# Block 0 of a fused S5 and GEGLU kernel: tile 3 moved last and read from its DMA-turned form, the last weight chunk split by columns over two DMA queues

## The chip, the cores and the metric

The kernel runs on one core of a Trainium2 chip. The metric is the device time of one execution in microseconds, the median of several runs. A profile of one execution adds a span, from the first to the last instruction, which is a little shorter than that execution's device time.

The core has five engines that run side by side and meet at semaphores: TensorE (PE, matmuls; its weight loads are listed as PEld), VectorE (DVE), ScalarE (ACT), GpSimd (POOL) and SyncE (SP), which here does nothing but issue DMAs. ScalarE can issue DMAs as well. Each issuing engine has its own queue; 16 DMA engines move the packets.

## The reference

```
xn = layernorm(x)                                  # x: 2048 x 512, bf16
Lam_bar = exp(dt * Lam);  B_bar = ((Lam_bar - 1) / Lam)[:, None] * B
Bu = xn @ B_bar.T;  h[t] = Lam_bar * h[t-1] + Bu[t]           # complex, 512 states
y  = 2 * real(h @ C.T) + xn * Dskip
g  = (gelu(xn @ w_gate) * (xn @ w_up)) @ w_down    # 512 -> 1376 -> 512
out = x + y + g
```

## The kernel before

The 2048 rows are worked in four blocks of 512 rows, a block in four tiles of 128 rows. For each block there are these stages on TensorE: GU (gate and up products, L843, and L817 for the last 96 columns), BU (input to the states, L749), DN (down product and states to output, L885). VectorE does the recurrence (scans), ScalarE evacuates PSUM, applies gelu and makes the tables.

TensorE contracts over the partition dimension, so a normalized tile must be turned (rows and columns exchanged) before it is used. There are two ways in this kernel. `TR` (L733 to L738) issues a DMA transpose per tile from SyncE: `XN[tile]` becomes columns 128j to 128j+127 of `XNT[block]`, and the buffers `XTk[block][j]` stand for that in the dependency tracking. `cent_T` (L678 to L689) turns a tile on TensorE with an identity matrix and ScalarE copies it out of PSUM into `XC_all`; it is used in block 0 alone, where there is no time to wait for DMAs.

Block 0's start is special. The tiles are only centred (mean subtracted; `cent` for tiles 0 and 1, `sub` for 2 and 3), turned by `cent_T`, and multiplied with the weights before the row's scale is known. The scale 1/std is applied later, as a per-row scalar, when PSUM is evacuated (`GT_evac`: a gelu with `scale=sc` on ScalarE, then a product with the scalar `sc` on VectorE, giving rows of `H0`). Here rows are on partitions: the tile is the stationary operand, and gate and up columns of both weights stream together (`WGU`). The columns 0 to 895 are cut in four units u, `FR = ((0,256),(256,512),(512,768),(768,896))`. For units 0 and 1 of tiles 0 to 2, `GT_k` (L701) adds one row block k of the weights at a time, in the order in which these land. The remaining ten pairs (j, u) of tile and unit are whole groups, `GT_mm` (L712), in an order written out by hand at L1013: (3,0), (3,1), (0,2), (0,3), (1,2), (1,3), (2,2), (2,3), (3,2), (3,3), each with a PSUM bank of its own from a second list. Each is followed by its `GT_evac`. Later `H0_T` turns `H0` by DMA. Columns 896 to 1375 of block 0 (ft 7 to 10) are done by `GU(0, [7, 8, 9, 10], halved=[7])` on the DMA-turned tiles; ft 7 is cut in halves over the tiles (0, 1 and 2, 3), so that its first half needs only two of the turns. `norms` (L634) makes the fully normalized tiles for these turns on VectorE.

The weights `WG` and `WU` come in column chunks `FC = [(0,512), (512,896), (896,1376)]`. The first chunk is loaded by row blocks k (`ld_wk`, L488, eight copies of 128 rows). The others are one copy for each matrix, with 512 packets (`ld_w`, L493). `wdeps` maps a column tile ft to the chunk it has to wait for.

The order on SyncE at the start is: x tiles and first weight chunk, second weight chunk, third weight chunk, a small transpose of the parameters (`tr_par`, L515), the four turns of block 0 (L736), x of block 1 (L482), turns of B_re and B_im straight from memory (L526), the Dskip row (L535), x of block 2 (L482), the turns of block 1 (L736), and so on.

All instructions are recorded with their buffers, and a list scheduler (`Sched`) orders VectorE, ScalarE and GpSimd by a cost model. TensorE and SyncE are kept in the recorded order. `order_behind` ties one instruction behind another on the same engine. `next_bank` deals out the eight PSUM banks in turn; `rstate["n"]` is its counter.

Of the kernel before, what the change touches and what calls it, by code (L numbers as in the profile page):

```python
# [9 lines left out]
ALU = mybir.AluOpType  # L10
ACTF = mybir.ActivationFunctionType
# [350 lines left out]
def d_act(n, ptr=0): return 190.0 + 0.833 * n + 90.0 * ptr  # L362
# [3 lines left out]
def build(nc, ins, out):  # L366
    with ExitStack() as es:
# [13 lines left out]
        assert WG.lo == 0 and WU.lo == WG.hi  # L381
        WGU = arena_t[:, 0:2 * KD * F].rearrange("p (w k f) -> p w k f", w=2, k=KD)
        WD = A.alloc("WD", [KF, D], BF16)
        FC = [(0, 512), (512, 896), (896, F)]
        WGc = [Buf("WGc%d" % i, "sbx", 10 * i, 10 * i + 1) for i in range(KD + 2)]
        WUc = [Buf("WUc%d" % i, "sbx", 100 + 10 * i, 101 + 10 * i) for i in range(KD + 2)]
        wdeps = lambda Wc, ft: Wc[0:KD] if ft < 4 else [Wc[KD + (ft > 6)]]
        WDc = [Buf("WDc%d" % i, "sbx", 200 + 10 * i, 201 + 10 * i) for i in range(2)]
        XNT_all = A.alloc("XNT", [NB, KD, TB_], BF16)
        XNT = ring(XNT_all, "XNT", NB)  # L390
# [100 lines left out]
        def ld_w(W, Wc, src, n):  # L491
            f0, f1 = FC[n]
            return S.dma(lambda e: e.dma_start(W.ap[:, :, f0:f1], src[:, f0:f1].rearrange("(k p) f -> p k f", p=128)),  # L493
                         1024 * (f1 - f0), writes=[Wc[KD + n - 1]], tag="ld_w")
# [5 lines left out]
        for k in range(KD):  # L500
# [1 line left out]
                ld_x0(k)  # L502
            ld_wk(WG, WGc, ins["B_w_gate"], k)
            ld_wk(WU, WUc, ins["B_w_up"], k)
        ld_w(WG, WGc, ins["B_w_gate"], 1)
        ld_w(WU, WUc, ins["B_w_up"], 1)

        def load_par():
            for q, nm in enumerate(("A_log_dt", "A_Lambda_re", "A_Lambda_im")):
# [17 lines left out]
                      1.4 * 512 * 1024, writes=[b_], tag="tr_" + nm, issue=3000.0)  # L527

        def load_W():
            ld_w(WG, WGc, ins["B_w_gate"], 2)  # L530
            ld_w(WU, WUc, ins["B_w_up"], 2)

        def load_B():
            load_T([A.sub(BBT_all, "BBTc%d" % c, c) for c in range(2)], ("A_B_re", "A_B_im"))
# [169 lines left out]
        def GT_mm(j, u, bank):  # L704
            f0, f1 = FR[u]
            w = f1 - f0
            dst = PS[bank][:, 0:2 * w].rearrange("p (w f) -> p w f", w=2)

            def f(e):
                ins_ = None  # L710
                for k in range(KD):
                    ins_ = e.matmul(dst, XCd(j, k), WGU[:, :, k, f0:f1], start=(k == 0), stop=(k == KD - 1))  # L712
                return ins_
            PE(f, d_pe([2 * w] * KD), wdeps(WGc, 2 * u) + wdeps(WUc, 2 * u) + XCs[j], [BANK[bank]], "GT")

        def GT_evac(j, u, bank):
            f0, f1 = FR[u]
            w = f1 - f0
            GATE["nh"] = kk = (GATE["nh"] + 1) % 3
            sc, rb = rss[j]  # L720
            GATE["last_gelu"] = S.order_behind(ACT(lambda e: e.activation(GG[kk].ap[:, 0:w], PS[bank][:, 0:w], ACTF.Gelu_apprx_tanh, scale=sc),  # L721
                                                   d_act(w, 1), [BANK[bank], rb], [GG[kk]], "gelu"), GATE.get("last_gelu"))
            hp = Buf("H0_%d_%d" % (j, u), "sb", H0[j].lo + 2 * f0, H0[j].lo + 2 * f1)
            GATE["hm"] = S.order_behind(V(lambda e: e.scalar_tensor_tensor(H0[j].ap[:, f0:f1], PS[bank][:, w:2 * w], sc, GG[kk].ap[:, 0:w], ALU.mult, ALU.mult),  # L724
                                          d_dve_1x(w), [BANK[bank], GG[kk], rb], [hp], "hmul"), GATE.get("hm"))

        def H0_T():
            for j in range(4):
# [77 lines left out]
        def GU_rest(b):  # L806
            k2, ft = b % 2, KF - 1
            f0, m = 128 * ft, FROWS[ft]
            for i in range(2):
                bank = next_bank()  # L810

                def f(e, i=i, bank=bank):
                    ins_ = None
                    for j in (2 * i, 2 * i + 1):
                        dst = PS[bank][:, 256 * (j % 2):256 * (j % 2) + 2 * m].rearrange("p (w f) -> p w f", w=2)
                        for dk in range(KD):
                            ins_ = e.matmul(dst, XNT[b].ap[:, dk, 128 * j:128 * (j + 1)], WGU[:, :, dk, f0:f0 + m],  # L817
                                            start=(dk == 0), stop=(dk == KD - 1))
                    return ins_
                PE(f, d_pe([2 * m] * 8), [WGc[KD + 1], WUc[KD + 1]] + XTr(b), [BANK[bank]], "GR%d" % b)  # L820
# [171 lines left out]
        ch(*stats(0, 1))  # L992
        op, mn0, qb0, rq0 = root(0, 0, 3)
        ch(op)
        ch(*stats(0, 3)); ch(sub(3))
        ch(recip(qb0, rq0))
        op, mn3, qb3, rq3 = root(0, 3, 4)
        ch(op)
        rss = [(rq0.ap[:, i:i + 1], rq0) for i in range(3)] + [(rq3.ap, rq3)]
        for j in range(2):  # L1000
            ch(norms(0, [j], mn0, rq0, 0))
        ch(recip(qb3, rq3))
        TR(0, [0, 1])
# [107 lines left out]
```

## Time and profile before

| what | value |
|---|---|
| median of 3 runs | 177.13 us (177.06 to 177.36) |
| the profiled execution: its time | 177.26 us |
| its span | 175.9 us |
| granted TensorE clock | 1.000 |
| bytes moved by DMA | 14.36 MB in 32421 packets |

In the lines of the profile an engine's name with a q (SPq, ACTq) marks the issue of a DMA. The duration of such a row is how long the issue held the engine's queue, not how long the transfer took. A row of the timeline gives start, duration, engine, source line, operation, output and input, count, and in brackets the idle time ahead of it with what ended it. "arena" is the one SBUF allocation in which all buffers lie, so "arena<-arena" with DMA_TRANSPOSE is a turn within SBUF. The matmul durations of the profile overlap each other: consecutive 512-column matmuls start 0.216 us apart, 256-column ones 0.109 us.

### The profile page before, as it was taken

The page shows a single profiled execution, that of the slowest core. Times are in us where ns is not written, and L with a number is a line of the kernel's source. Part 1 is how long each engine was busy: PE and PEld are TensorE (multiplying, and loading weights), DVE is VectorE, ACT ScalarE, POOL GpSimd, SP SyncE. Part 2 cuts the span into 40 slices and gives each one's busy share as a digit, 9 for nine tenths or more (in the row PEclk, how much of TensorE's full clock was granted, in tenths as well). Part 3 has the DMA queues.
Part 4 walks back from the last instruction along what each step waited for, and adds up shares of the span by engine and source line. Part 5 has one row for each costly group of instructions (what it writes and reads, how often), then busy time and mean ns, then how long its engine had stood idle before and what let it go on. Part 6 is the DMA issues. An engine that isn't in the chain of part 4 may idle for free.

```text
span 175.9 us, 2549 instructions
## 1 busy us (share of the span) xinstructions
PE 172.8 (98%) x903; PEld 85.4 (49%) x903; DVE 159.7 (91%) x279; ACT 95.8 (54%) x187; POOL 10.7 (6%) x24
## 2 busy tenths in 40 slices
PE   7999999999999999999999999999999999999995
PEld 2645664744544444444644444444464444444454
DVE  6797999987999989889899999989999899999941
ACT  5367668999766899383676793000667970000000
POOL 3132120211000000002200000000000000000000
DMA  5999989975899000002015000002004000000311
GB/s 144 281 322 154 216 136 203 174 132 114 162 270 270 11 0 2 0 30 75 18 33 112 5 0 4 0 0 89 30 0 34 0 0 0 0 0 4 119 62 60
DMA packets 32421, 14.36 MB, mean 82 GB/s; under 512 B 23737, under 2 KB 32409, under 8 KB 32409
## 3 DMA queue, kind: packets, MB, share of 16 engines
q1 hardware_dynamic: 31952, 13.84, 36.9%
q10 hardware_dynamic: 456, 0.36, 0.6%
q8 instruction: 7, 0.11, 0.3%
q14 instruction: 6, 0.04, 0.1%
HBM read 6.46 MB, written 2.10 MB: 49 GB/s over the span
## 4 chain that ended last, share of the span: by engine, by line
PE 95%; DMA 2%; SPq 1%; issue 0%; DVE 0%
PE PS L885 37%; PE PS L843 32%; PE PS L749 16%; PE PS L712 4%; PE PS L817 3%; PE PS L701 2%; DMA arena<-in_B_w_up_dram 2%; SPq L488 1%; PE PS L684 0%; SPq L497 0%; DVE arena L903 0%
## 5 line engine op out<-in xcount | busy, mean ns | idle before, releaser
L885 PE MATMUL PS<-arena 128*128 128x512 bf16 (+3 forms) x323 | 66.2, 366 | 0.0
L843 PE MATMUL PS<-arena 128*128 128x512 bf16 (+1 forms) x272 | 58.1, 373 | 0.0
L885 PEld LDWEIGHTS PS<-arena 128*128 128x128 bf16 (+1 forms) x323 | 30.8, 98 | 35.2
L843 PEld LDWEIGHTS PS<-arena 128*128 128x128 bf16 x272 | 26.5, 98 | 29.5
L787 DVE TENSOR_TENSOR_SCAN arena<-arena 128x512 bf16<-128x512 f32 x32 | 38.9, 1256 | 0.0
L859 ACT ACTIVATE arena<-PS 128x512 bf16<-128x512 f32 x33 | 19.8, 599 | 26.2 <-DVE arena L903 16.7
L749 PE MATMUL PS<-arena 128*128 128x512 bf16 (+1 forms) x144 | 28.3, 355 | 0.1
L863 ACT ACTIVATE arena<-PS 128x512 bf16<-128x512 f32 x33 | 19.8, 599 | 5.4 <-PE PS L843 5.4
L749 PEld LDWEIGHTS PS<-arena 128*128 128x128 bf16 x144 | 14.0, 98 | 13.7 <-DMA arena<-arena 0.6
L877 ACT ACTIVATE PS<-arena 128x512 f32<-128x512 bf16 (+2 forms) x17 | 9.6, 582 | 19.7 <-DVE arena L903 19.0
L758 ACT ACTIVATE arena<-PS 128x512 bf16<-128x512 f32 x32 | 17.6, 597 | 1.6 <-PE PS L749 1.6
L903 DVE TENSOR_TENSOR arena<-PS,arena 128x512 bf16<-128x512 f32 (+2 forms) x17 | 10.9, 654 | 6.4 <-PE PS L885 6.4
L865 DVE TENSOR_TENSOR arena<-arena 128x512 bf16<-128x512 bf16 x33 | 13.2, 419 | 2.1 <-ACT arena L863 2.0
L776 DVE TENSOR_TENSOR arena<-arena 128x4096 bf16<-128x4096 bf16 (+1 forms) x5 | 9.2, 1859 | 0.4 <-ACT arena L611 0.4
L799 DVE TENSOR_TENSOR arena<-arena 128x4096 bf16<-128x4096 bf16 x4 | 9.2, 2291 | 0.1
L774 DVE TENSOR_TENSOR arena<-arena 128x4096 bf16<-128x4096 bf16 (+1 forms) x5 | 9.2, 1861 | 0.0
L800 DVE TENSOR_TENSOR arena<-arena 128x4096 bf16<-128x4096 bf16 x4 | 9.1, 2287 | 0.0
L615 DVE BATCH_NORM_STATS2 arena<-arena 128x6 f32<-128x512 bf16 x12 | 7.8, 685 | 0.9 <-DMA arena<-in_A_x_dram 0.7
L721 ACT ACTIVATE arena<-PS,arena 128x256 bf16<-128x256 f32 (+1 forms) x16 | 6.5, 450 | 3.3 <-DVE arena L621 1.5
L712 PE MATMUL PS<-arena 128*128 128x512 bf16 (+1 forms) x40 | 7.1, 336 | 0.0
L701 PE MATMUL PS<-arena 128*128 128x256 bf16 (+1 forms) x36 | 6.2, 308 | 0.2 <-DMA arena<-in_B_w_up_dram 0.2
L724 DVE SCALAR_TENSOR_TENSOR arena<-PS,arena 128x256 bf16<-128x256 f32 (+1 forms) x16 | 6.2, 444 | 0.0
(95 smaller groups left out, 124.2 us busy)
## 6 DMA issues: line engine op xcount, KB each, us to landing
out_dram<-arena SPq DMA_DIRECT2D x15, 128.0 KB, 1.7
arena<-in_A_x_dram SPq DMA_DIRECT2D x3, 512.0 KB, 6.3
arena<-in_B_w_down_dram SPq DMA_DIRECT2D x1, 1280.0 KB, 8.8
arena<-in_B_w_gate_dram SPq DMA_DIRECT2D x4, 128.0 KB, 3.4
arena<-in_B_w_up_dram SPq DMA_DIRECT2D x4, 128.0 KB, 3.6
arena<-in_B_w_gate_dram SPq DMA_DIRECT2D x1, 480.0 KB, 6.8
arena<-in_B_w_up_dram SPq DMA_DIRECT2D x1, 480.0 KB, 7.6
arena<-arena SPq DMA_TRANSPOSE x25, 3.3
```

What stands on the lines that cost most here:

```text
L701: PE(lambda e: e.matmul(dst, XCd(j, k), WGU[:, ws[0]:ws[-1] + 1, k, f0:f1], start=first, stop=k == KD - 1, skip_group_check=True), d_pe([w ...
L712: ins_ = e.matmul(dst, XCd(j, k), WGU[:, :, k, f0:f1], start=(k == 0), stop=(k == KD - 1))
L749: ins_ = e.matmul(PS[bank][:, 128 * j0:128 * j1], BBT[c][dk].ap[:, 128 * s:128 * (s + 1)], XNT[b].ap[:, dk, 128 * j0:128 * j1], start=(dk ...
L758: GATE["evBu"] = ACT(lambda e, bank=bank, k3=k3, s=s, c=c: e.activation(SSc[k3][s][c].ap, PS[bank][:, :], ACTF.Copy), d_act(512), [BANK[ba ...
L787: V(lambda e, g=g, rb=rb, init=init: e.tensor_tensor_scan(g.ap, rb, g.ap, init, ALU.mult, ALU.add), d_dve_scan(512), [g, PA[RRr]] + ([CARc ...
L843: ins_ = e.matmul(PS[bank][0:m, c0:c1], W.ap[:, dk, 128 * ft:128 * ft + m], XNT[b].ap[:, dk, c0:c1], start=(dk == 0), stop=(dk == KD - 1))
L859: GATE["last_gelu"] = ACT(lambda e, bg=bg, kk=kk, m=m: e.activation(GG[kk].ap[0:m, :], PS[bg][0:m, :], ACTF.Gelu_apprx_tanh), d_act(512), ...
L863: ACT(lambda e, bu=bu, kk=kk, m=m: e.activation(UPB[kk].ap[0:m, :], PS[bu][0:m, :], ACTF.Copy), d_act(512), [BANK[bu]], [UPB[kk]], "evU")
L865: V(lambda e, kk=kk, m=m, ft=ft, k2=k2: e.tensor_tensor(HTt[k2][ft].ap[0:m, :], GG[kk].ap[0:m, :], UPB[kk].ap[0:m, :], ALU.mult), d_dve_tt ...
L877: ACT(lambda e: e.activation(PS[bank][:, c0:c1], X[tt].ap[:, c0:c1], ACTF.Copy), d_act(c1 - c0), [X[tt]], [BANK[bank]], "seed")
L885: ins_ = e.matmul(PS[bank][:, c0:c1], l_[:, 128 * j:128 * (j + 1)], r_[:, c0:c1], start=False, stop=last and n == len(ops) - 1, skip_group ...
L903: V(lambda e: e.tensor_tensor(OUTB[ko].ap[:, c0:c1], PS[bank][:, c0:c1], XD[tt].ap[:, c0:c1], ALU.add), d_dve_1x(c1 - c0), [BANK[bank], XD ...
```

## The change

In block 0 tile 3 is no longer centred and turned on TensorE. It is normalized fully, turned by DMA, and its four groups read it from `XNT[0]` at the end of the order; so its gelu and product take no scale. The order of the ten groups becomes (0,2), (1,2), (2,2), (0,3), (1,3), (2,3), (3,0), (3,1), (3,2), (3,3), with other banks. The DMA turns of block 0 are issued in the order 0, 3, 1, 2. The weight columns from 512 on are cut in four chunks instead of two: 512 to 767, 768 to 895, 896 to 1023, 1024 to 1375. The first three are loaded from SyncE ahead of the small transpose and the turns (six copies, where there were four); the last, of both matrices, is issued from ScalarE's queue behind the gelu of group (2,2).

```diff
-        FC = [(0, 512), (512, 896), (896, F)]
+        FC = [(0, 512), (512, 768), (768, 896), (896, 1024), (1024, F)]
-        wdeps = lambda Wc, ft: Wc[0:KD] if ft < 4 else [Wc[KD + (ft > 6)]]
+        wdeps = lambda Wc, ft: Wc[0:KD] if ft < 4 else [Wc[KD + (ft > 5) + (ft > 6) + (ft > 7)]]
...
-        ld_w(WG, WGc, ins["B_w_gate"], 1)
-        ld_w(WU, WUc, ins["B_w_up"], 1)
+        for n in (1, 2):
+            ld_w(WG, WGc, ins["B_w_gate"], n)
+            ld_w(WU, WUc, ins["B_w_up"], n)
...
         def load_W():
-            ld_w(WG, WGc, ins["B_w_gate"], 2)
-            ld_w(WU, WUc, ins["B_w_up"], 2)
+            ld_w(WG, WGc, ins["B_w_gate"], 3)
+            ld_w(WU, WUc, ins["B_w_up"], 3)
...
                 for k in range(KD):
-                    ins_ = e.matmul(dst, XCd(j, k), WGU[:, :, k, f0:f1], start=(k == 0), stop=(k == KD - 1))
+                    xs = XCd(j, k) if j < 3 else XNT[0].ap[:, k, 128 * j:128 * (j + 1)]
+                    ins_ = e.matmul(dst, xs, WGU[:, :, k, f0:f1], start=(k == 0), stop=(k == KD - 1))
                 return ins_
-            PE(f, d_pe([2 * w] * KD), wdeps(WGc, 2 * u) + wdeps(WUc, 2 * u) + XCs[j], [BANK[bank]], "GT")
+            PE(f, d_pe([2 * w] * KD), wdeps(WGc, 2 * u) + wdeps(WUc, 2 * u) + (XCs[j] if j < 3 else [XT0[j]]), [BANK[bank]], "GT")
...
+            if j < 3:
+                sc, rb = rss[j]
+                fg = lambda e: e.activation(g, gate, ACTF.Gelu_apprx_tanh, scale=sc)
+                fh = lambda e: e.scalar_tensor_tensor(h, up, sc, g, ALU.mult, ALU.mult)
+                rb = [rb]
+            else:
+                fg = lambda e: e.activation(g, gate, ACTF.Gelu_apprx_tanh)
+                fh = lambda e: e.tensor_tensor(h, up, g, ALU.mult)
+                rb = []
...
-        ch(*stats(0, 3)); ch(sub(3))
-        ch(recip(qb0, rq0))
+        ch(*stats(0, 3))
         op, mn3, qb3, rq3 = root(0, 3, 4)
         ch(op)
-        rss = [(rq0.ap[:, i:i + 1], rq0) for i in range(3)] + [(rq3.ap, rq3)]
-        for j in range(2):
-            ch(norms(0, [j], mn0, rq0, 0))
+        ch(recip(qb0, rq0))
+        rss = [(rq0.ap[:, i:i + 1], rq0) for i in range(3)]
+        ch(norms(0, [0], mn0, rq0, 0))
+        ch(norms(0, [1], mn0, rq0, 0))
         ch(recip(qb3, rq3))
-        TR(0, [0, 1])
+        ch(norms(0, [3], mn3, rq3, 3))
+        TR(0, [0, 3, 1])
...
         for j in range(3):
             GT_k(3, j, 0, [0, 1])
-            if j == 0:
-                cent_T(3, 0, 4, 6)
...
-        for (j, u), bank in zip([(3, 0), (3, 1), (0, 2), (0, 3), (1, 2), (1, 3), (2, 2), (2, 3), (3, 2), (3, 3)],
-                                (6, 7, 0, 1, 2, 3, 4, 5, 0, 7)):
+        for (j, u), bank in zip([(0, 2), (1, 2), (2, 2), (0, 3), (1, 3), (2, 3), (3, 0), (3, 1), (3, 2), (3, 3)],
+                                (6, 7, 0, 1, 2, 3, 4, 5, 6, 7)):
             GT_mm(j, u, bank)
             GT_evac(j, u, bank)
-        rstate["n"] = 2
+            if (j, u) == (2, 2):
+                o = S.order_behind(ld_w(WG, WGc, ins["B_w_gate"], 4, "scalar"), GATE["last_gelu"])
+                GATE["last_gelu"] = S.order_behind(ld_w(WU, WUc, ins["B_w_up"], 4, "scalar"), o)
+        rstate["n"] = 0
         norms(0, [2], mn0, rq0, 0)
-        norms(0, [3], mn3, rq3, 3)
-        TR(0, [2, 3])
+        TR(0, [2])
```

In the built program TensorE's order differs only in block 0: the four transposes are gone and the 40 matmuls of `GT_mm` stand in the new order. SyncE issues two copies more ahead of the small transpose, ScalarE two copies behind nine gelus. VectorE's order changes around it: the product groups of units 3 and of tile 3 now stand behind the first parameter product (L558), which waits for the small transpose and a GpSimd instruction.

More of the change, by code (lines that the diff above doesn't have):

```diff
@@ L383, in build @@
         WD = A.alloc("WD", [KF, D], BF16)
-        FC = [(0, 512), (512, 896), (896, F)]
-        WGc = [Buf("WGc%d" % i, "sbx", 10 * i, 10 * i + 1) for i in range(KD + 2)]
-        WUc = [Buf("WUc%d" % i, "sbx", 100 + 10 * i, 101 + 10 * i) for i in range(KD + 2)]
-        wdeps = lambda Wc, ft: Wc[0:KD] if ft < 4 else [Wc[KD + (ft > 6)]]
+        FC = [(0, 512), (512, 768), (768, 896), (896, 1024), (1024, F)]
+        WGc = [Buf("WGc%d" % i, "sbx", 10 * i, 10 * i + 1) for i in range(KD + 4)]
+        WUc = [Buf("WUc%d" % i, "sbx", 100 + 10 * i, 101 + 10 * i) for i in range(KD + 4)]
+        wdeps = lambda Wc, ft: Wc[0:KD] if ft < 4 else [Wc[KD + (ft > 5) + (ft > 6) + (ft > 7)]]
         WDc = [Buf("WDc%d" % i, "sbx", 200 + 10 * i, 201 + 10 * i) for i in range(2)]
@@ L489, in ld_wk, with ld_w @@
                          256 * (f1 - f0), writes=[Wc[k]], tag="ld_w")
-        def ld_w(W, Wc, src, n):
+        def ld_w(W, Wc, src, n, queue="sync"):
             f0, f1 = FC[n]
             return S.dma(lambda e: e.dma_start(W.ap[:, :, f0:f1], src[:, f0:f1].rearrange("(k p) f -> p k f", p=128)),
-                         1024 * (f1 - f0), writes=[Wc[KD + n - 1]], tag="ld_w")
+                         1024 * (f1 - f0), writes=[Wc[KD + n - 1]], tag="ld_w", queue=queue)
         def ld_x0(j, queue="sync", after=()):
@@ L719, in GT_evac @@
             GATE["nh"] = kk = (GATE["nh"] + 1) % 3
-            sc, rb = rss[j]
-            GATE["last_gelu"] = S.order_behind(ACT(lambda e: e.activation(GG[kk].ap[:, 0:w], PS[bank][:, 0:w], ACTF.Gelu_apprx_tanh, scale=sc),
-                                                   d_act(w, 1), [BANK[bank], rb], [GG[kk]], "gelu"), GATE.get("last_gelu"))
             hp = Buf("H0_%d_%d" % (j, u), "sb", H0[j].lo + 2 * f0, H0[j].lo + 2 * f1)
-            GATE["hm"] = S.order_behind(V(lambda e: e.scalar_tensor_tensor(H0[j].ap[:, f0:f1], PS[bank][:, w:2 * w], sc, GG[kk].ap[:, 0:w], ALU.mult, ALU.mult),
-                                          d_dve_1x(w), [BANK[bank], GG[kk], rb], [hp], "hmul"), GATE.get("hm"))
+            gate, up, g, h = PS[bank][:, 0:w], PS[bank][:, w:2 * w], GG[kk].ap[:, 0:w], H0[j].ap[:, f0:f1]
+            if j < 3:
[7 more added lines that the diff above has]
+                rb = []
+            GATE["last_gelu"] = S.order_behind(ACT(fg, d_act(w, 1), [BANK[bank]] + rb, [GG[kk]], "gelu"), GATE.get("last_gelu"))
+            GATE["hm"] = S.order_behind(V(fh, d_dve_1x(w), [BANK[bank], GG[kk]] + rb, [hp], "hmul"), GATE.get("hm"))
         def H0_T():
@@ L819, in f @@
                     return ins_
-                PE(f, d_pe([2 * m] * 8), [WGc[KD + 1], WUc[KD + 1]] + XTr(b), [BANK[bank]], "GR%d" % b)
+                PE(f, d_pe([2 * m] * 8), [WGc[KD + 3], WUc[KD + 3]] + XTr(b), [BANK[bank]], "GR%d" % b)
                 GATE["nh"] = kk = (GATE["nh"] + 1) % 3
```

## The prediction

> **What bounds the kernel now.** I read the page's busy table, then the chain of waits in order of time, then TensorE's waits, and last SyncE's timeline, because the change rearranges DMAs. Measured against no change, about 0.2% (0.35 us) is what a measurement of this kernel can tell.
>
> ```profile
> PE 172.8 (98%) x903; PEld 85.4 (49%) x903; DVE 159.7 (91%) x279; ACT 95.8 (54%) x187; POOL 10.7 (6%) x24
> ```
>
> TensorE is occupied for all but 3 us. From 6.32 us on, the chain that ends last is TensorE's own work:
>
> ```profile
> 9.75 0.34 PE PS L684 x4
> 10.09 1.08 PE PS L701 x5
> 11.16 6.93 PE PS L712 x40
> ...
> 24.61 6.91 PE PS L749 x32
> 31.52 0.12 issue
> 31.64 7.11 PE PS L749 x48
> ```
>
> The first row holds the four transposes of tile 3 that the change drops. The row "issue" at 31.52 is small but decides the case: there TensorE has finished BU(0) and is about to start BU(1). TensorE's weight loads in the timeline around it say what it waits for:
>
> ```profile
> 31.61 1.44 PEld L749 LDWEIGHTS PS<-arena 128*128 128x128 bf16 x14 [0.58 <-DMA arena<-arena]
> ```
>
> So BU(1) begins on a DMA turn of block 1. Its first halves read tiles 0 and 1 of the block; the turn of tile 1 is issued at 26.62 and, in the DMA view of 26.6 to 27.8 us, lands 4.9 us later:
>
> ```profile
> arena<-arena SPq DMA_TRANSPOSE x1, 4.9
> ```
>
> 26.62 + 4.9 = 31.5, and the matmul starts at 31.64. TensorE is therefore just ahead of this transfer, with no slack. What stands in front of it on SyncE's queue is shown in the timeline (start, duration of the issue):
>
> ```profile
> 5.47 0.43 SPq L493 DMA_DIRECT2D arena<-in_B_w_gate_dram  x1
> 5.95 0.51 SPq L493 DMA_DIRECT2D arena<-in_B_w_up_dram  x1
> 6.50 0.51 SPq L493 DMA_DIRECT2D arena<-in_B_w_gate_dram  x1
> 7.04 0.65 SPq L493 DMA_DIRECT2D arena<-in_B_w_up_dram  x1
> 7.82 1.99 SPq L515 DMA_TRANSPOSE arena<-arena  x1
> 10.27 5.15 SPq L736 DMA_TRANSPOSE arena<-arena  x4
> 15.46 0.58 SPq L482 DMA_DIRECT2D arena<-in_A_x_dram  x1
> 16.09 3.22 SPq L526 DMA_TRANSPOSE arena<-in_A_B_re_dram  x1
> 19.35 3.67 SPq L526 DMA_TRANSPOSE arena<-in_A_B_im_dram  x1
> 23.07 0.58 SPq L535 DMA_DIRECT2D arena<-in_A_Dskip_dram  x1
> 23.69 0.43 SPq L482 DMA_DIRECT2D arena<-in_A_x_dram  x1
> 24.17 6.34 SPq L736 DMA_TRANSPOSE arena<-arena  x4
> ```
>
> From 10.27 on every issue starts within 0.1 us of the end of the one before: the queue never waits for data. The only slack is 0.46 us ahead of 10.27, where it waits for VectorE's normalized tile 0 (L634, ends 10.24). Whatever delays SyncE before 10.27 by more than that moves everything behind it, up to the turn that TensorE waits for.
>
> **The change part by part.** *Tile 3's transposes go.* The matmul before them would have handed over at 9.59 (9.37 plus the 0.216 step of a 512-column matmul); the next L701 starts at 9.92. That is 0.34 us of TensorE: 0.22 for four steps of 56 ns, 0.10 of waiting for the subtraction on VectorE (L951, 0.35). With them go that subtraction and one ScalarE copy (L689, 0.59), both off the path. So L712 can start at 11.00 - 0.34 = 10.66.
>
> *The order of L712.* The 40 matmuls are the same. But (0,2) now comes first, without the 1.73 us of (3,0) and (3,1) ahead of it, and needs columns 512 to 767 of both weights. Weights of the last row block land at 4.98 + 3.8 = 8.78; then 2 x 512 packets of 512 bytes follow. Packets per us, in the DMA views of 8.5 to 9.5 (768 bytes) and of 19 to 20 (256 bytes):
>
> ```profile
> DMA packets 376, 0.28 MB, mean 280 GB/s; under 512 B 12, under 2 KB 376, under 8 KB 376
> ```
>
> ```profile
> DMA packets 1115, 0.29 MB, mean 285 GB/s; under 512 B 1115, under 2 KB 1115, under 8 KB 1115
> ```
>
> So 42.6 ns and 14.3 ns of one of 16 engines; 28 ns between them. 1024 x 28 / 16 = 1.8 us, landing 10.6; scaling the two old chunks by bytes, 2/3 of 3.2 us, gives 10.9. TensorE waits 0 to 0.3 us; I take 0.24, start 10.9.
>
> *Two more copies on SyncE ahead of the turns.* Four become six, each of 512 packets as before, only narrower. Price from below: the issue alone, 0.48 us a piece, 0.96. From above: the copy of x at 15.46 and the issue behind it. L526 took 3.22 there and, for the same shape with no copy before it (C_re), 2.44; so the copy held the queue until 16.09 + 0.78 = 16.87, 1.41 us; two are 2.8. Between: from 5.47 to the end of the small transpose at 9.81 are 4.34 us for four copies and it, at most 1.08 a copy. Below zero: if the 1.99 us of L515 is a wait for bytes in flight, fewer bytes ahead (1.0 MB for 1.73) shorten it to the size of a plain issue and the six copies cost nothing. I take 1.0 a copy, the row nearest to what is added. L515 then ends at 9.81 + 2.0 = 11.8; the first turn starts at 11.86 instead of 10.27: **+1.6 us** for the queue (bounds 0 and +2.4).
>
> *The turns, order 0, 3, 1, 2.* Each issue takes 1.27 to 1.31, and a turn that finds the engines free lands 2.5 us after its issue. Tile 3: 11.86 + 1.31 + 2.5 = 15.7. TensorE reaches (3,0) at 10.9 + 12 x 0.216 + 3 x 0.433 = 14.8: a new wait of 0.9, and everything behind it on TensorE waits too. The four tile-3 groups take 3 x 0.864 + 0.433 = 3.03, so GU(0) starts at 18.7 instead of 17.93: +0.8. Tile 1 lands at 17.0 and tile 2 at 18.3; GU(0) needs them at 18.7 and 19.6. Hidden.
>
> *The rest of the last chunk on ScalarE's queue.* Issued behind the gelu of (2,2): TensorE ends that group at 13.5, so about 13.8 and 14.3. Like the copy of x (4.1 us to landing) they land near 18 and 18.9; ft 8 needs them at 18.7 + 1.73 = 20.4 and 21.3. About 2 us of cover. Behind the two issues (0.27 to 0.57 each on ScalarE) wait the gelus of (0,3), (1,3), (2,3), whose banks 1 to 3 are wanted again from 18.7 on. Hidden. VectorE now stands at L558 before those products, until the small transpose has landed and GpSimd's 1.0 us is over (L558 started at 16.27 before; I leave it there). Four steps of 1.3 us together (L558 to L602) and then three products of 0.34 follow, so the first, in bank 1, ends near 17.9; GU(0) wants that bank at 18.7 + 0.44 = 19.1. Hidden by 1.2 us. Gelu and product of tile 3 without a scale, and its normalization, cost what they did.
>
> *What the queue's delay does later.* The x load, both B turns, the skip row, the next x load and block 1's turns all issue 1.6 later. B_re lands at 23.65 + 1.6 = 25.25, BU(0) starts at 24.45 + 0.8 = 25.25: just in time. Tile 1 of block 1 lands at 31.55 + 1.6 = 33.15, where TensorE arrives at 32.3. So the 0.8 us of lag grows to 1.6 at BU(1), and behind it TensorE has no idle to give back.
>
> **Sum.** -0.34 + 0.24 + 0.9 = +0.8 by GU(0), then +0.8 at BU(1): +1.6. The profiled execution had 177.26 us (span 175.9), which gives 178.9; the median of the runs, 177.13, is 0.13 lower: **178.7 us**.
>
> **The rivals.**
> 1. *Issues alone* (0.20). Copies cost 0.48 each: +0.96 less the 0.46 of slack, +0.5: 177.6. For it: no issue of L493 is over 0.65. Against: every transpose issued behind copies is long (1.99; 2.41 for the first turn at 24.17, where its like take 1.27).
> 2. *The queue isn't late* (0.16). L515 shrinks with the bytes ahead of it, the first turn stays at VectorE's 10.24, and BU(1) still starts on a landing at 31.55. TensorE comes 0.34 sooner and waits 0.46: 177.1.
> 3. *Faster* (0.13). As 2, and with emptier engines the chain from the x load to block 1's turns runs ahead by at least 0.46, so TensorE keeps 0.34 and loses the 0.12 of idle: 176.7. It decides from tile 1 landing before 31.1. For it: the two B turns pause (under 0.1 of the engines' share in parts of 22 to 24 us), so the chain isn't rigid. Against: it begins with SyncE's issues, which don't come sooner.
> 4. *ScalarE's copies get in SyncE's way* (0.10). Their two preparations, 1.0 each, delay SyncE's turns too: +3.6, 180.7. For it: between 13.8 and 16 both queues issue. Against: no row here shows both queues with large copies. The Trainium skill, "DMA: Bandwidth & Descriptors", section "Queues, rings and completion order", says that SP's and ACT's rows are rings on the same 16 engines and no descriptor generator of their own; by that rule this rival would hold. No run so far shows it.
> 5. *Narrow packets cost like wide ones* (0.05). 2048 packets at 42.6 instead of 14.3 ns are 3.6 us more: the last weights land near 16.4, tile 3 at 17.4, TensorE +2.6: 179.7. The row of 19 to 20 us (1115 packets of 256 bytes in 1 us) is against it, though these are transposes. The same page, section "Specifications", states that transfers under 512 bytes are read, modified and written; by that rule the packets would be slow. The trace's row doesn't agree.
>
> **How the numbers follow.** The forecast has 0.36. Slower by over 0.2%: 0.36 + 0.20 + 0.10 + 0.05 = 0.71; within: 0.16; faster: 0.13. The range takes in rivals 1, 2, 4 and 5 and leaves out 3 and what lies beyond 4: 177.0 to 180.9. The slower side alone, rivals 1 and 5 and the forecast, is 177.5 to 179.8.
>
> **What would show it.** L515 ending near 11.8 and the first turn issued near 11.9 (10.8 for rival 1, 10.2 for 2 and 3). TensorE idle ahead of (3,0), about 0.9, on a DMA within the arena; a second such wait near 32.3. The x load issued at 17.05. No wait of ft 8 for weights. Wrong would be: an x load at 15.5 or earlier, or block 1's tile 1 landing before 31.5.

## The result, and the profile after

| | before | after |
|---|---|---|
| median (17 runs each) | 177.08 us | 178.44 us |
| lowest, highest | 176.68, 177.54 | 177.62, 181.93 |
| ratio, 95% interval | | 1.0075, 1.0057 to 1.0093 |
| profiled execution: time, span | 177.26, 175.9 | 177.74, 176.4 |

The changed kernel is 0.75% slower, and it scatters more. Two of its runs (181.45 and 181.93) stand outside the ratio, with a granted TensorE clock under 1; the other 15 lie between 177.62 and 179.41. The profiled execution is one of the quicker ones: it shows 0.48 us of the 1.36 by which the medians differ. Line numbers have moved by up to nine: L745 is the turn of a tile, L714 the tile-by-tile matmul of block 0, L852 and L826 are GU, L758 is BU.

First SyncE's and ScalarE's issues, from the timeline of the changed kernel (start, duration of the issue):

```profile
7.60 0.86 SPq L493 DMA_DIRECT2D arena<-in_B_w_gate_dram  x1
8.50 0.91 SPq L493 DMA_DIRECT2D arena<-in_B_w_up_dram  x1
9.53 1.18 SPq L516 DMA_TRANSPOSE arena<-arena  x1
10.75 5.20 SPq L745 DMA_TRANSPOSE arena<-arena  x4
13.71 0.41 ACTq L493 DMA_DIRECT2D arena<-in_B_w_gate_dram  x1
14.15 0.64 ACTq L493 DMA_DIRECT2D arena<-in_B_w_up_dram  x1
16.00 0.59 SPq L482 DMA_DIRECT2D arena<-in_A_x_dram  x1
```

The two added copies hold the queue for 1.8 us, but the small transpose behind them is shorter (1.18 for 1.99) and the slack ahead of the first turn is used up. The first turn goes out at 10.75 instead of 10.27, the x load at 16.00 instead of 15.46. SyncE is late by 0.5 us, not by 1.6.

Next TensorE, in the same timeline:

```profile
10.57 7.25 PE L714 MATMUL PS<-arena 128*128 128x512 bf16 x40
14.61 2.92 PEld L714 LDWEIGHTS PS<-arena 128*128 128x128 bf16 x16 [0.26 <-DMA arena<-arena]
17.79 1.03 PE L852 MATMUL PS<-arena 128*128 128x256 bf16 x8
19.25 4.50 PE L852 MATMUL PS<-arena 128*128 128x256 bf16 x24 [0.44 <-DMA arena<-arena]
32.05 3.84 PEld L758 LDWEIGHTS PS<-arena 128*128 128x128 bf16 x35 [0.46 <-DMA arena<-arena]
```

The tile-by-tile matmuls start 0.43 us sooner than before (11.00) and hardly wait for tile 3 (row of 14.61). GU(0) still starts sooner than before, at 17.79. After its first eight matmuls it waits: the row of 19.25 reads the second halves, which need tile 2 of block 0. This wait is new. The wait of the weight loads ahead of BU(1) at 32.05 is no longer than before (0.46 for 0.58).

The chain of waits says what the new wait hangs on:

```profile
13.36 1.27 SPq L745
14.63 0.04 issue
14.68 4.54 DMA arena<-arena
19.21 0.04 issue
19.25 4.50 PE PS L852 x24
```

It is the turn of tile 2: issued at 14.68, on the ground 4.54 us later. The DMA view of 14.65 to 14.9 us gives what was issued beside it (kilobytes, time from issue to landing; the first was issued at 14.15 and is listed as still being issued):

```profile
arena<-in_B_w_up_dram ACTq DMA_DIRECT2D x1, 352.0 KB, 4.4
arena<-arena SPq DMA_TRANSPOSE x1, 4.5
```

A turn that finds the engines free lands 2.5 us after its issue; the turns of tiles 0 and 3 did (2.51 and 2.52). The turn of tile 1, issued at 13.36, took 4.23 and landed at 17.59; that of tile 2 took 4.54; the x load took 5.74 instead of 4.06 and landed at 21.74 instead of 19.52. All three were in flight together with ScalarE's two copies.

TensorE's milestones, from the starts of these groups in both traces:

| TensorE | before | after | shift | shift in the prediction |
|---|---|---|---|---|
| tile-by-tile matmuls start | 11.00 | 10.57 | -0.43 | -0.10 |
| GU(0) starts | 17.93 | 17.79 | -0.14 | +0.8 |
| last 96 columns of GU(0) start | 23.13 | 23.59 | +0.46 | |
| BU(0) starts | 24.45 | 25.00 | +0.55 | +0.8 |
| GU(1) starts | 38.58 | 39.02 | +0.44 | +1.6 |
| end of the span | 175.9 | 176.4 | +0.5 | +1.6 |

So the whole loss of this execution arises between 17.8 and 23.6 us, at one wait. By the starts of the matmuls that wait costs 0.60 us (18.55 to 19.25, where the step is 0.11); the 0.44 of the row counts from the modelled end of the matmul before. The lag at GU(1) is then -0.43 at the start, +0.29 ahead of tile 3's groups, +0.60 at tile 2, +0.09 ahead of BU(0) and -0.11 at BU(1): +0.44.

### The profile page after: what moved, and what is told of

Read it like the earlier page. It is cut to its first block, busy times and chain, and to the rows that moved or that the text cites. A ratio compares the mean times of both kernels' runs of the same rounds, so it can differ in the third digit from the quotient of the medians.

```text
span 176.4 us, 2548 instructions
## 1 busy us (share of the span) xinstructions
PE 173.1 (98%) x899; PEld 85.2 (48%) x899; DVE 159.4 (90%) x278; ACT 94.6 (54%) x186; POOL 11.7 (7%) x24
## 4 chain that ended last, share of the span: by engine, by line
PE 88%; DMA 3%; DVE 1%; SPq 1%; issue 0%; DVEq 0%
PE PS L894 37%; PE PS L852 32%; PE PS L758 16%; PE PS L826 3%; DMA arena<-arena 3%; DVE arena L727 1%; SPq L745 1%; DVE arena L912 0%; DVEq L341 0%
## 5 line engine op out<-in xcount | busy, mean ns | idle before, releaser
L852 PE MATMUL PS<-arena 128*128 128x512 bf16 (+1 forms) x272 | 58.3, 373 | 0.4 <-DMA arena<-arena 0.4
L852 PEld LDWEIGHTS PS<-arena 128*128 128x128 bf16 x272 | 26.4, 98 | 30.3 <-DMA arena<-arena 0.7
L758 PE MATMUL PS<-arena 128*128 128x512 bf16 (+1 forms) x144 | 28.3, 355 | 0.0
L758 PEld LDWEIGHTS PS<-arena 128*128 128x128 bf16 x144 | 13.9, 98 | 13.7 <-DMA arena<-arena 0.5
L912 DVE TENSOR_TENSOR arena<-PS,arena 128x512 bf16<-128x512 f32 (+2 forms) x17 | 10.9, 653 | 6.7 <-PE PS L894 6.7
L714 PE MATMUL PS<-arena 128*128 128x512 bf16 (+1 forms) x40 | 7.2, 337 | 0.0
L726 ACT ACTIVATE arena<-PS,arena 128x256 bf16<-128x256 f32 (+1 forms) x12 | 4.5, 447 | 3.0 <-PE PS L702 1.5
L596 DVE SCALAR_TENSOR_TENSOR arena<-arena 128x512 bf16<-128x512 bf16 x8 | 5.5, 745 | 0.6 <-ACT arena L593 0.6
```

What stands on the lines that cost most here:

```text
L758: ins_ = e.matmul(PS[bank][:, 128 * j0:128 * j1], BBT[c][dk].ap[:, 128 * s:128 * (s + 1)], XNT[b].ap[:, dk, 128 * j0:128 * j1], start=(dk ...
L852: ins_ = e.matmul(PS[bank][0:m, c0:c1], W.ap[:, dk, 128 * ft:128 * ft + m], XNT[b].ap[:, dk, c0:c1], start=(dk == 0), stop=(dk == KD - 1))
L912: V(lambda e: e.tensor_tensor(OUTB[ko].ap[:, c0:c1], PS[bank][:, c0:c1], XD[tt].ap[:, c0:c1], ALU.add), d_dve_1x(c1 - c0), [BANK[bank], XD ...
```

## The experiments

Two theories stood against each other. QUEUE is the prediction's: the two extra copies make SyncE late, and the lateness reaches TensorE at BU(1). CROWD: the two copies on ScalarE's queue delay the turns and the x load that are in flight beside them, and the cost arises in GU(0). Times are medians; ratios are to the kernel before on the same chip and at the same time (177.08 us for the first four below; 176.91 for the loads alone, the copies one group later and the narrow tail; 177.10 for the rest), with 95% intervals.

**The changed kernel again.** No edit.

> The changed kernel unaltered, for a second profile and its spread. Two theories of its loss. QUEUE (the forecast's): SyncE issues late behind six copies, and TensorE waits for block 1's turn at BU(1). CROWD: ScalarE's two copies run on the same DMA engines as the turns of tiles 1 and 2 and the x load, and these land late. Both expect about 178.4. QUEUE expects the x load issued at 16.0 or later and landing about 4.1 us after its issue, and TensorE's longest wait at BU(1) near 32. CROWD expects the turn of tile 2 to land over 4 us after its issue (2.5 when the engines are free), the x load over 5 us after its issue, and TensorE's longest wait in GU(0) near 18.7.

178.18 us, 1.0063 [1.004, 1.0085]. The loss repeats. The execution that was profiled took 181.49 us, far above the median, and shows the same collision at a higher price:

```profile
20.77 6.96 PE L852 MATMUL PS<-arena 128*128 128x256 bf16 x32 [2.67 <-DVE arena L605]
```

GU(0) starts at 20.77, 2.8 us later than in the kernel before. The row names VectorE's L605, but that had ended at 20.22; the turn of tile 1, which these matmuls read, landed only at 20.57. It was issued at 13.64, 0.03 us behind ScalarE's gate copy, and took 6.93 us; tile 2 took 5.88 and the x load 6.60. TensorE's longest wait stands in GU(0), as CROWD expects, and not at BU(1).

**Four copies on SyncE instead of six.**

```diff
-        FC = [(0, 512), (512, 768), (768, 896), (896, 1024), (1024, F)]
+        FC = [(0, 512), (512, 768), (768, 1024), (1024, F)]
...
```

> Columns 768 to 1023 in one chunk: four copies on SyncE instead of six, with the same bytes ahead of the turns; ScalarE's copies as they are. The first turn goes back to 10.25, the x load to 15.5 (0.5 earlier). QUEUE expects the loss to go with it: 177.1 to 177.5. CROWD expects the turns of tiles 1 and 2 to be crossed all the same (tile 2 landing over 4 us after issue) and most of the loss to stay: 178.0 to 178.5.

177.71 us, 1.0039 [1.0026, 1.0052]. SyncE is on time again: the first turn goes out at 9.96, the x load at 15.16. About half of the loss is gone, and half stays. TensorE's waits and, below, the chain of waits of this run:

```profile
PE PS L851 <- DMA arena<-arena: 0.5, 1, 0.5
```

```profile
13.84 5.38 DMA arena<-arena
```

The wait is the same one as in the changed kernel (L851 is GU here): tile 2, issued 0.16 us behind ScalarE's gate copy, landed 5.38 us later. No wait is left at BU(1). With QUEUE alone nothing would have been left to pay, except 0.2 us that TensorE waits ahead of (0,2) for its weights. Tile 1, issued 1.15 us ahead of the gate copy, was on time here (2.54 us): an earlier queue also brings one more turn out of the copies' way, so that not all of the half that is gone need be QUEUE's.

**The last chunk from SyncE, behind the four turns.** ScalarE issues no weights.

```diff
-            if (j, u) == (2, 2):
-                o = S.order_behind(ld_w(WG, WGc, ins["B_w_gate"], 4, "scalar"), GATE["last_gelu"])
-                GATE["last_gelu"] = S.order_behind(ld_w(WU, WUc, ins["B_w_up"], 4, "scalar"), o)
...
         TR(0, [2])
+        ld_w(WG, WGc, ins["B_w_gate"], 4)
+        ld_w(WU, WUc, ins["B_w_up"], 4)
```

> The last chunk (columns 1024 to 1375 of both) issued from SyncE behind the four turns instead of from ScalarE's queue; all else as in the changed kernel. CROWD expects the turns of tiles 1 and 2 to land 2.5 us after issue again and the wait in GU(0)'s second halves to go; the x load now stands behind two copies. If CROWD's part is the larger: 177.5 to 178. QUEUE expects the two copies, 0.5 to 1.0 each on the queue, to go straight into BU(1): 179 to 180.5.

178.7 us, 1.0105 [1.0076, 1.0135]. All four turns land 2.46 to 2.53 us after their issue, and TensorE doesn't wait for them any more. But the x load is issued only at 16.94, and B_re, behind it on the queue, lands at 26.14. TensorE's waits:

```profile
PE PS L758 <- DMA arena<-in_A_B_re_dram: 1.5, 1, 1.5
PE PS L852 <- DMA arena<-in_B_w_gate_dram: 0.2, 1, 0.2
```

Without ScalarE's copies the turns are punctual: for CROWD. A late queue does cost, as QUEUE says, though the wait stands at BU(0), for B_re, and not at BU(1). The time lies between what the two theories had expected (177.5 to 178, and 179 to 180.5).

**Tile 3 alone.** The order of the groups, the turns and tile 3's form as in the change; chunks and queues as before.

```diff
-        FC = [(0, 512), (512, 768), (768, 896), (896, 1024), (1024, F)]
+        FC = [(0, 512), (512, 896), (896, F)]
...
         def load_W():
-            ld_w(WG, WGc, ins["B_w_gate"], 3)
-            ld_w(WU, WUc, ins["B_w_up"], 3)
+            ld_w(WG, WGc, ins["B_w_gate"], 2)
+            ld_w(WU, WUc, ins["B_w_up"], 2)
...
-            if (j, u) == (2, 2):
-                o = S.order_behind(ld_w(WG, WGc, ins["B_w_gate"], 4, "scalar"), GATE["last_gelu"])
-                GATE["last_gelu"] = S.order_behind(ld_w(WU, WUc, ins["B_w_up"], 4, "scalar"), o)
```

> Tile 3's part alone: order of groups, turn order and tile 3 from its turned form as in the changed kernel; chunks and queues of the kernel before. No late queue and no copies on ScalarE, so neither theory's loss. (0,2) now waits for the old second chunk (landing 11.95, 1.3 us of wait), the group (3,0) comes at 15.9 just behind tile 3's landing (15.65), GU(0) starts near 18.9, 1.0 later than before: 178.0 to 178.2, all of it from the wait ahead of (0,2).

177.77 us, 1.0044 [1.0028, 1.006]. TensorE's waits show one new row:

```profile
PE PS L713 <- DMA arena<-in_B_w_up_dram: 0.7, 1, 0.7
```

(0,2) is now the first group, and the wide chunk 512 to 895 lands only at 11.58. So the narrow chunk 512 to 767 does its work in the changed kernel (landed 10.33, no wait). The cause is the expected one, at about half the price: a wait of 1.3 us and 178.0 to 178.2 had been expected.

**The loads alone.** The kernel before with the change's chunks and queues; ScalarE's copies behind (0,2), the third of its ten groups, as (2,2) is in the change.

```diff
-        FC = [(0, 512), (512, 896), (896, F)]
+        FC = [(0, 512), (512, 768), (768, 896), (896, 1024), (1024, F)]
...
+            if (j, u) == (0, 2):
+                o = S.order_behind(ld_w(WG, WGc, ins["B_w_gate"], 4, "scalar"), GATE["last_gelu"])
+                GATE["last_gelu"] = S.order_behind(ld_w(WU, WUc, ins["B_w_up"], 4, "scalar"), o)
```

> The loads' part alone: chunks, queues and ScalarE's copies as in the changed kernel (issued behind the third of the ten groups, near 13.8), tile 3 centred and turned on TensorE and first in the order, as before. CROWD: the turn that is issued near or behind ScalarE's copies lands over 4 us after its issue, GU(0)'s second halves wait 0.3 to 1: 177.6 to 178.4. Nothing of the loss is tile 3's. If the loads cost nothing without the new order: 177.1.

179.35 us, 1.0157 [1.0127, 1.0186]: dearer than the whole change, against all expectations. In this order ScalarE's gate copy goes out at 15.47 and not near 13.8, and the fourth turn is issued at 15.72, 0.25 us behind it. TensorE's waits and the chain of waits, of an execution of 181.09 us, the longest of the six:

```profile
PE PS L844 <- DMA arena<-arena: 3.1, 1, 3.1
```

```profile
15.72 7.12 DMA arena<-arena
```

The same collision, with a turn that took 7.12 us; the third turn, issued 1.50 us ahead of the copy, took 2.50. Not all of the loss is the copies': TensorE also waits 0.7 us for a product on VectorE (L725), which stands here behind a parameter step (L575) that starts only at 12.79, when the small transpose has landed (12.77). The two parts of the change don't add up (1.0044 and 1.0157 alone, 1.0075 together): tile 3's part alone pays for a wide chunk that the loads' part makes narrow, and what the loads cost depends on which turn the copies meet.

**The copies one group later.** Once on the changed kernel, once with the four copies of above.

```diff
-            if (j, u) == (2, 2):
+            if (j, u) == (0, 3):
```

> The changed kernel with ScalarE's two copies behind the gelu of (0,3) instead of (2,2): issued near 15.1 and 15.6 instead of 13.7 and 14.15, so behind the last turn's issue (14.7). CROWD, in the form that copies and turns are served in the order of their issue: the turns of tiles 1 and 2 land 2.5 to 2.8 us after issue, TensorE's 0.4 of wait in GU(0)'s second halves goes; the last weights land near 18.7 and 20.3 (ft 8 needs them at 19.4 and 20.3), x and B_re late as before. 177.7 to 178.1 against 178.4 of the changed kernel. QUEUE: SyncE's issues are as in the changed kernel, so 178.2 to 178.5.

> e2 (four copies on SyncE) and e5 (ScalarE's copies behind the last turn's issue) together. CROWD: turn of tile 2 lands near 16.5, GU(0) runs through; left are 0.2 of wait ahead of (0,2), and B_re (near 24.6) against BU(0) at 24.3. 177.0 to 177.4, about even with the kernel before. If the turns land late all the same, CROWD in this form falls: 177.6 to 177.8, as e2.

178.16 us, 1.0068 [1.005, 1.0086], and 177.88, 1.0057 [1.0037, 1.0078]. The first missed its aim: VectorE's order changed with it, and the copies (14.11, 14.55) still went out ahead of the last turn (15.08), which landed 5.98 us later. Its profiled execution, of 179.34 us, is the longest of the six and waits longer at the same place, in TensorE's waits:

```profile
PE PS L852 <- DMA arena<-arena: 1.8, 1, 1.8
```

In the second, tile 2 was issued at 13.58, 0.65 us ahead of the gate copy. In the trace's packet records 494 of its 512 packets had started by 15.5 and the rest by 16.0, yet it landed at 17.4 to 19.4 from one DMA engine to the next, each about 0.2 behind the gate copy there (17.2 to 19.2). Its packets had run; its completion came only behind the copy's. Well behind the copies it is otherwise: in the changed kernel tile 2, issued 0.97 us behind the gate copy, had only one of its own packets started by 17.75, when 949 of the copies' 1024 had. 177.88 us is also a little above both values that had been expected (177.0 to 177.4 with CROWD, 177.6 to 177.8 without).

**A narrow tail.** 32 columns (64 KB in all) on ScalarE instead of 352, in the same 1024 packets of 64 bytes; SyncE takes 896 to 1343.

```diff
-        FC = [(0, 512), (512, 768), (768, 896), (896, 1024), (1024, F)]
+        FC = [(0, 512), (512, 768), (768, 896), (896, 1344), (1344, F)]
...
```

> The changed kernel with columns 896 to 1343 loaded from SyncE ahead of the turns and only 32 columns (1344 to 1375) of both left to ScalarE: its two copies keep their 2 x 512 packets but have 64 KB instead of 704. If bytes on the DMA engines delay the turns of tiles 1 and 2, these land 2.5 to 3 us after their issue. If it is the number of packets, that is the preparing of the descriptors one copy after the other, the turn that is issued behind the copies is still 1.5 us or more late (over 4 us after issue). The weights ahead of the turns are 640 KB more, so tile 3's turn lands near 15.5 and TensorE waits about 0.9 ahead of (3,0): 177.9 to 178.8 by either.

177.43 us, 1.0037 [1.0023, 1.005]: better than expected. Tile 1, issued 0.11 us ahead of the gate copy, still took 3.63 us and landed (17.18) just behind the up copy (16.87). With an eleventh of the bytes some 1.1 us of delay is left, where the changed kernel's two profiles have 1.7 and 4.4 for this turn. So the delay doesn't go in step with the bytes; that they don't matter isn't shown, since the small copies also landed sooner (2.3 and 2.8 us after issue, for 3.7 and 4.4) and the turn with them. Tile 2 landed by 17.47 on 15 DMA engines and at 19.20 on the last; a 16 KB instruction packet ran on one engine from 17.0 to 18.0, which may be the reason. TensorE waits 0.5 us ahead of (3,0), for the 0.9 expected.

**The copies behind the last turn.** In the changed kernel behind (3,0), as shown; then with the four copies of above behind (2,3).

```diff
-            if (j, u) == (2, 2):
+            if (j, u) == (3, 0):
```

> The changed kernel with ScalarE's two copies behind the gelu of (3,0): issued near 16.4, over a microsecond behind the end of the last turn's issue (15.95 in the changed kernel) and behind the x load's. CROWD: the turns of tiles 1 and 2 now both land 2.5 to 2.7 us after their issue and TensorE's wait in GU(0)'s second halves goes; but the weights come late, behind x, near 20.5 and 22, and TensorE waits 1 to 2 us at ft 8: 178.5 to 179.5. If the turns land over 4 us after issue without any copy near them, CROWD is wrong. QUEUE: SyncE's issues are unchanged, 178.4.

> Four copies on SyncE (as e2) and ScalarE's copies behind the gelu of (2,3): issued near 15.0 and 15.5, just behind the end of the last turn's issue (14.85) and beside the x load's. CROWD: the turn of tile 2 lands by 17.0, its packets and its completion ahead of the copies, so GU(0)'s second halves don't wait; the weights land near 18.7 and 20.3, a wait of up to 0.5 at ft 8 at most. 177.1 to 177.6. If the completion of tile 2's turn is again held until the gate copy's landing (as its packets in e6 were through by 15.6 and it landed at 19.4): 177.7 to 178.0.

181.92 us, 1.0255 [1.0219, 1.0291], and 180.2, 1.0147 [1.0126, 1.0167]. Both show the turns of tiles 1 and 2 on time (2.49 and 2.49; 2.55 and 2.50), as CROWD says. But now the copies meet the x load and the turn of B_re, and are themselves late. The DMA view of 16.2 to 16.9 us of the first, and TensorE's waits of the second:

```profile
arena<-in_A_x_dram SPq DMA_DIRECT2D x1, 512.0 KB, 6.8
arena<-in_B_w_gate_dram ACTq DMA_DIRECT2D x1, 352.0 KB, 5.7
arena<-in_B_w_up_dram ACTq DMA_DIRECT2D x1, 352.0 KB, 7.5
```

```profile
PE PS L851 <- DMA arena<-in_B_w_up_dram: 1.9, 1, 1.9
```

GU(0) then waits for weights instead of for a tile. The sizes were missed by far: 178.5 to 179.5 us had been expected of the first, 177.1 to 177.6 of the second. In the first a part is TensorE's clock, as the last section shows.

**BU(1)'s slack.** The kernel before, with block 2's x load moved behind block 1's turns.

```diff
-            ld_x(2)
...
         TR(1)
+        ld_x(2)
```

> The kernel before with the x load of block 2 issued behind block 1's turns instead of ahead of them; nothing else. The forecast held that TensorE's start of BU(1) hangs on these turns without slack. If so, they land over 1 us earlier and the 0.12 us of idle ahead of BU(1) goes: 176.9 to 177.0, not to be told from 177.1. If a SyncE queue that is 1 us earlier there moves nothing, or VectorE waits longer for x of block 2: 177.1 or more. It tells how much slack BU(1) can be given, so whether the queue could have carried the change.

177.3 us, 1.0007 [0.9997, 1.0016]. Tile 1 of block 1 lands at 27.97 instead of 31.55, and the small idle time ahead of BU(1) is gone; the time stays. So the place on which the prediction built its second half can be given 3.5 us of slack, and in the kernel before that is worth nothing that can be measured.

The turns nearest to ScalarE's copies, in the order of the gap between the issues of turn and gate copy. The last column says which of ScalarE's two copies had landed just before the turn, and how long before:

| run | turn issued | gate copy issued | copy behind turn by | turn landed after | lands behind |
|---|---|---|---|---|---|
| changed kernel again, tile 2 | 14.96 | 13.61 | -1.35 | 5.88 | up, 0.63 |
| narrow tail, tile 2 | 14.86 | 13.65 | -1.21 | 2.6 (one engine 4.33) | up, 0.6 |
| changed kernel, tile 2 | 14.68 | 13.71 | -0.97 | 4.54 | up, 0.63 |
| copies one group later, tile 2 | 15.08 | 14.11 | -0.97 | 5.98 | up, 0.47 |
| loads alone, fourth turn | 15.72 | 15.47 | -0.25 | 7.12 | up, 0.23 |
| four copies, tile 2 | 13.84 | 13.68 | -0.16 | 5.38 | up, 0.24 |
| changed kernel again, tile 1 | 13.64 | 13.61 | -0.03 | 6.93 | up, 0.37 |
| narrow tail, tile 1 | 13.54 | 13.65 | 0.11 | 3.63 | up, 0.30 |
| changed kernel, tile 1 | 13.36 | 13.71 | 0.35 | 4.23 | gate, 0.17 |
| copies one group later, tile 1 | 13.76 | 14.11 | 0.35 | 4.34 | gate, 0.18 |
| four copies and (0,3), tile 2 | 13.58 | 14.23 | 0.65 | 5.82 | gate, 0.20 |
| four copies, tile 1 | 12.54 | 13.68 | 1.15 | 2.54 | |
| four copies and (2,3), tile 2 | 14.23 | 15.43 | 1.20 | 2.50 | |
| copies behind (3,0), tile 2 | 14.96 | 16.27 | 1.30 | 2.49 | |
| loads alone, third turn | 13.97 | 15.47 | 1.50 | 2.50 | |

From 1.15 us ahead of the copies on a turn is on time; no run lies between that and 0.65. Nearer than that, or behind them, it lands just behind a copy: behind the gate copy when it was issued 0.35 to 0.65 us ahead of it, behind the up copy when it was issued later. How late it is follows from when that copy lands. The second row alone is hardly late: there the small copies had landed by 16.87.

None of these kernels beat the one before. Of those with the change, the nearest are the narrow tail and the four copies.

## Why the prediction was right, and where it wasn't

The forecast of 178.7 us lies 0.26 above the median, and the sign is right. That it lies so near is luck: the price of SyncE's queue was taken too high, the delay of the turns beside ScalarE's copies was left out, and the two errors offset each other. The two signs of being wrong that the prediction named didn't come either (x load at 16.00, block 1's tile 1 at 31.99): they asked only for a queue that isn't late at all, and couldn't tell 0.5 us from 1.6. Its other signs could: the first turn at 10.75 is the first rival's 10.8 and not the forecast's 11.9.

*Tile 3's transposes and the order of the matmuls*: right, and better than forecast. The start moved by -0.43 for -0.10, since the narrow chunk landed at 10.33 and the 0.24 us of waiting taken from 10.6 to 10.9 didn't come. "Tile 3 alone" shows the same wait at 0.7 where the chunk is wide.

*Two more copies on SyncE at 1.0 us each, "+1.6 us for the queue"*: this step failed. The measured shift is 0.49 for the first turn and 0.54 for the x load: the size of the first rival, issue alone less the slack. The small transpose ends at 10.71 instead of 9.81, so a copy cost 0.45 and not 1.0. The choice of 1.0 shared the long issue of the small transpose out among the copies, as if each further copy made it longer still. It doesn't: whatever stands fifth on the queue takes long (in all profiles 1.57 to 2.27 us as the transpose, 0.84 to 1.69 as a copy), and with six copies that is a copy.

| kernel | copies ahead | fifth issue | small transpose | it ends at | first turn issued |
|---|---|---|---|---|---|
| before | 4 | the transpose | 1.99 | 9.81 | 10.27 |
| four copies | 4 | the transpose | 1.97 | 9.69 | 9.96 |
| changed | 6 | 0.86 | 1.18 | 10.71 | 10.75 |
| narrow tail | 6 | 1.25 | 1.18 | 10.89 | 10.94 |

Nor is it the bytes, as the prediction's lower bound had it: "four copies" moves the same bytes ahead of the small transpose as the changed kernel and has 1.97, the narrow tail moves 640 KB more and has 1.18. Over all profiles the first turn goes out at 9.69 to 10.35 behind four copies and at 10.54 to 11.36 behind six, so this shift too scatters, and the 0.49 is one of its small values; 11.86 is outside in any case. What makes the fifth issue long isn't shown.

*The new wait of 0.9 ahead of (3,0)*: fell with it. Tile 3 landed at 14.57 instead of 15.7; TensorE's weight load shows 0.26 there, and the groups begin 0.29 late.

*"Tile 1 lands at 17.0 and tile 2 at 18.3 ... Hidden"*: this step failed for tile 2, and in the second profile for tile 1 too. Tile 2 landed at 19.21, although its issue was 0.5 us behind the old place and not 1.6. The step "ScalarE's copies ... Hidden" had asked only whether the copies arrive in time for ft 8, and there it was right (17.42 and 18.58, no wait for weights). It hadn't asked what the copies do to the turns and the x load in flight beside them. The table of turns answers that: those that meet the copies take 3.6 to 7.1 us, those that don't 2.5. This is the direction of the fourth rival, at a smaller price and at another spot: it had SyncE's issues delayed by 2 us, while behind the copies each turn's issue still took 1.28 us and the landings came late. (The issue of B_re's turn took 4.56 us for 3.22; in "tile 3 alone", without ScalarE's copies, it took 4.52, so that isn't shown to be theirs.)

For that rival the prediction had the rule of the Trainium skill, "DMA: Bandwidth & Descriptors", section "Queues, rings and completion order", that both queues are rings on the same 16 engines. The traces agree as far as turns on SyncE's queue land behind copies on ScalarE's. The Trainium skill says in the same section that the increment of the semaphore lands only after every earlier write from that engine, across its queues. The turn in "four copies and (0,3)" that landed 0.2 us behind the copy on each engine, its packets long through, fits this; the runs don't test the mechanism itself.

*The chain from the x load to BU(1), shifted rigidly by 1.6*: failed. The x load landed 2.2 us late, but tile 1 of block 1 landed at 31.99 instead of 31.55, 0.44 late, and BU(1) began with no more idle time than before. The lag on the way shows where it was given back: B_im's turn landed 1.26 us late, the skip row behind it only 0.30. Between 21 and 26 us the engines of the kernel before have two microseconds with almost nothing to move (18 GB/s from 21 to 22, 22 from 25 to 26; in the changed kernel 126 and 290), so the pauses that rival 3 pointed to are the likely place; no run tests it. Where this chain does bite is B_re: it landed at 24.95 and BU(0) started at 25.00, and in "the last chunk from SyncE" BU(0) waited 1.5 us for it. "BU(1)'s slack" adds that the idle time ahead of BU(1) is worth nothing that can be measured in the kernel before.

*VectorE's, ScalarE's and the banks' cover*: right; TensorE waited for no bank and no product.

What stays open: the profiled execution carries 0.48 us of the 1.36 at the median. The second profile, at 181.49 us, waits 2.67 in GU(0), and a near twin at 179.34 us has 1.8 at the place of the 0.44; so the scatter is likely that of where the copies meet the turns and when they land. No profile of the changed kernel at its median time was taken that shows it.

## What to carry to other kernels

A copy that is moved to another issuing queue isn't out of the way: look at what is in flight when it is issued, and check the landing times of those transfers as well as its own. Short transfers on which an engine waits should be issued well ahead of a large copy (here 1.15 us was enough, 0.65 was not). A long issue may belong to its place in the queue and not to the transfer that stands there: compare two kernels with different transfers in that place before sharing it out. Before building a forecast on a chain of transfers, look for the places in it that take up a delay.

## What was unexpected of the hardware

A copy issued 0.65 us after a turn, on another queue, still held up the turn's landing by 3.3 us (5.82 for 2.5). Every late turn landed 0.17 to 0.63 us behind one of the copies. Even copies of 64 KB in all, in 1024 packets of 64 bytes, held a turn by 1.1 us.

Narrow packets from memory weren't dear. The median time of one was 18 ns at 256 bytes, 27 at 512, 34 at 704 and 46 at 1024; the six copies of the changed kernel had all landed by 12.16. Per byte the 256-byte packets are the dearest, but a packet takes about 8.5 ns plus 0.0365 ns a byte at all four sizes (worked out from these medians), with no step below 512 bytes. The rule of the Trainium skill, "DMA: Bandwidth & Descriptors", section "Specifications", that transfers under 512 bytes are read, modified and written, which the prediction weighed in its fifth rival, doesn't show in these loads.

A wait of TensorE can cost more than its length. In the run with the copies behind (3,0), TensorE waited 2.0 us at 20 and 1.3 us at 23 us, and the granted clock fell by half, in the trace's clock record from 23.41 to 30.23 us. Its windows (the third number from the right is the granted clock):

```profile
24.00:26.00 2.00, 1.61 (x4) 0.59 (x5) 1.97 (x7) 0.00 (x0) 0.88 (x2) 0.50 1.22 262
26.00:28.00 2.00, 2.00 (x6) 0.76 (x5) 1.96 (x10) 0.60 (x1) 1.19 (x2) 0.50 0.90 201
28.00:30.00 2.00, 2.00 (x8) 0.96 (x7) 2.00 (x6) 0.89 (x2) 0.00 (x0) 0.50 1.11 229
```

In "the changed kernel again" a wait of 2.7 us, up to 20.8, comes with a clock of 0.50 from 20.66 to 24.07; in "the loads alone" a wait of 3.1 us left it at 1.00. So the length of the gap doesn't decide it by itself. The two stretches at half clock are 6.83 and 3.41 us long, and the full clock ahead of each lasted 17.07 us: two, one and five times 3.41. In the 3.41 us ahead of the fall TensorE was idle for 2.35 and 2.56 us. The Trainium skill, "TensorE: Matmul & The Clock Gate", section "What's actually happening", describes a gate that halves the clock after an idle window of about 3.4 us, with windows that run free of the kernel's start. The steps of 3.41 us agree with that, and where a gap falls among them would be chance; but that 2.35 and 2.56 us of idleness in a window sufficed doesn't agree with a wholly idle one. Five of the six runs of the kernel with the copies behind (3,0) had a mean clock under 1; the one at 1.00 took 180.11 us.
